# Longformer attention and a StarReLU MLP on one core: K and Q turned by DMA transposes from batch 2 on, V's global rows by register-indexed casting loads

## The chip, the cores and the metric

The kernel runs on one core of one Trainium2 chip. The time is the device time of one launch in microseconds, given as the median over runs. The engines are named as in the profile: PE (TensorE matmul), PEld (its weight loads), DVE (VectorE), ACT (ScalarE), POOL (GpSimd) and SP (SyncE). SP computes nothing; it issues DMAs. POOL issues DMAs as well. PE's results land in PSUM, in the kernel's pools `ps_s`, `ps_o` and `ps_m`; all other tiles lie in SBUF.

## The reference

Attention over 8 batches x 8 heads x 576 positions x 64 dims, restricted to a band of 32 positions on each side and to 8 global positions, which see all and are seen by all. Its output is the input of a two-layer MLP with a squared ReLU.

```python
scores = (1 / sqrt(64)) * q @ k.T                 # q, k, v: (8, 8, 576, 64) float32
mask = (abs(i - j) <= 32) | is_global[i] | is_global[j]
attn = softmax(where(mask, scores, -1e9))
x = (attn @ v).transpose(0, 2, 1, 3).reshape(4608, 512)
r = maximum(x @ w_in, 0)                          # w_in: (512, 2048)
out = (s * r * r + b) @ w_out                     # w_out: (2048, 512), float32 out
```

## The kernel before

**Pairs and chunks.** Two heads of a batch form a *pair*; there are 32 pairs, four to a batch (`bi, hp = divmod(p, 4)`). The two heads lie in the two halves of 64 partitions. The 576 keys are cut into `NCH` = 5 chunks of `KC` = 120; ahead of each chunk stand the 8 global keys, so a chunk has 128 columns. A chunk's keys meet only the queries in the band around it, 160 or 192 columns per head (`LO`, `HI`, `W`), plus the global queries.

**K and Q before.** `load_kq` has POOL issue two casting DMAs per pair, which put six neighbouring rows on a partition (`six[t]`, bf16, a ring of `NR` = 6 pairs). `trans_a` (K) and `trans_b` (Q) turn them with 12 PE transposes each into a PSUM tile `pst` (L392). DVE copies K to `kt` (L403) and one half of Q to `qbd` (L416), ACT the other half of Q (L416). `put_kq` then writes the global columns, two small DVE copies (L375 into `kt`, L379 into `qbd`).

**V before.** `load_v` brings V's natural rows in float32 to `natv` (a ring of `NV` = 4 pairs), from POOL for the first pairs and from SP after that; `cast_v` rounds them into `vring` (ACT up to pair 7, POOL afterwards, L166). The 8 rows of each chunk that belong to the global keys are filled by `put_v` (DVE up to pair 7, POOL afterwards, L368) from `gvx`.

**Global rows before.** Once per two batches, `gather` has POOL issue three indirect DMAs (L228) that fetch the global rows of K, Q and V into `gf`. `globals_of` gives five steps for them: round K and Q to `gb` (L334), turn them on PE (L341, then L344 and L347 on DVE), round V (L352), and two steps `move`, in which 8 matmuls with slices of the identity bring V's rows to partitions 0 to 7 (L359, then the copy to `gvx`, L361).

**The order of the work.** The program is written out by hand: `tc.manual_schedule` keeps each engine's order as recorded, and the engines run in order. Pairs 0 to 3 go through `first_pair`. From pair 4 on `run_pair` takes a pair through eight steps. In each step the functions left in `later` by the step before are taken aside as `prev`, and at its end one *quantum* of the MLP is issued:

- steps 0 to 4: `qk` (scores on PE, L427; exp on ACT, L431; the product with the mask, `em`, on DVE, L434, left in `later`). Steps 1 and 3 also take one of the two normalising functions of the pair before (L484, L488 on ACT; L471 and L490 on DVE).
- step 6: `trans_a` and `trans_b` of the next pair, then `pv` (weighted V into `po` and row sums, L453), and `put_v` of the next pair.
- at the end of each step:

```python
            for f in extra.get(s, ()):
                f()
            for f in prev:
                f()
            Q(nq[s])
```

So an *extra* of a step is issued ahead of the functions left by the step before it. A quantum is either the psh matmuls of one 128-row block of the first layer (L523, then ReLU on ACT, L530, and the square on DVE, L533) or a quarter of a second-layer output tile (L538, with L552 or L549 on DVE and a store on SP after every fourth). 16 psh quanta and 16 pso quanta make one of nine tiles of 512 tokens. Two pairs of a batch carry psh quanta, two carry pso quanta, eight in each pair (six in pairs 4 to 7). What is left of the MLP runs after pair 31. `scatter` (POOL, L501) writes the global queries' outputs into `xt` once per batch. `wpiece` and the adds of L705 build a bias row in pairs 8 to 15, and `release` (L716) adds it to eight output tiles that were held back.

DMAs of one queue carry eight semaphores in turn, so that a DMA waits until the eighth before it on its queue has landed.

Of the kernel before, what the change touches and what calls it, by code (L numbers as in the profile page):

```python
# [9 lines left out]
FP32 = mybir.dt.float32  # L10
BF16 = mybir.dt.bfloat16
# [5 lines left out]
P = 128  # L17
B, H, S, D = 8, 8, 576, 64
NG = 8
# [8 lines left out]
NCH = 5  # L28
KC = 120
HB = 60  # L30
LQ = NCH * P
# [1 line left out]
HI = [P * c + P + WIN for c in range(NCH - 1)] + [LQ]  # L33
W = [HI[c] - LO[c] for c in range(NCH)]
NPAIR = B * H // 2
NR = 6
NV = 4
NJ = 6
NP6 = S // NJ
N6 = NCH * KC // NJ  # L40


# [8 lines left out]
def view(ap, *dims):  # L51

    return bass.AP(
        tensor=ap.tensor, offset=ap.offset, ap=[list(ap.ap[0])] + [list(d) for d in dims]
    )
# [8 lines left out]
def kernel(  # L64
# [12 lines left out]
    nc = tc.nc  # L77
# [5 lines left out]
    const = ctx.enter_context(tc.tile_pool(name="const", bufs=1))  # L83
# [5 lines left out]
    gpa = ctx.enter_context(tc.tile_pool(name="gpa", bufs=1))  # L89
    held = ctx.enter_context(tc.tile_pool(name="held", bufs=1))  # L90
    mop = ctx.enter_context(tc.tile_pool(name="mop", bufs=3))
    stage = ctx.enter_context(tc.tile_pool(name="stage", bufs=3))
    globp = ctx.enter_context(tc.tile_pool(name="globp", bufs=2))
    ps_s = ctx.enter_context(tc.tile_pool(name="ps_s", bufs=2, space=bass.MemoryType.PSUM))
    ps_o = ctx.enter_context(tc.tile_pool(name="ps_o", bufs=1, space=bass.MemoryType.PSUM))
# [11 lines left out]
            name=nc.get_next_instruction_name(), act_func_set_id=_set_id,  # L107
# [9 lines left out]
        out=gidx_p[:],  # L117
# [6 lines left out]
    src = {"k": k, "q": q, "v": v}  # L124

    six = {t: const.tile([P, NR, 2, NJ, D], BF16, name=f"six{t}", tag=f"six{t}") for t in "kq"}
    natv = const.tile([P, NV, NCH, 2, D], FP32)
    vring = const.tile([P, NV, NCH, 2, D], BF16)
    qbufs = [const.tile([P, 2, LQ], BF16, name=f"qbd{i}", tag=f"qbd{i}") for i in range(3)]
# [10 lines left out]
    def load_kq(p):  # L140
        bi, hp = divmod(p, 4)
        for t in "kq":
            nc.gpsimd.dma_start(  # L143
                out=six[t][:NP6, p % NR].rearrange("p h j d -> p h (j d)"),
                in_=src[t][bi, 2 * hp : 2 * hp + 2].rearrange("h (p j) d -> p h (j d)", j=NJ),
            )

    def load_v(eng, p):
        bi, hp = divmod(p, 4)
        for hh in range(2):  # L150
            o = v[bi, 2 * hp + hh, 0, 0].offset

            last = p == NPAIR - 1 and hh == 1
            for c, nch, n in ((0, NCH - 1, KC), (NCH - 1, 1, S - KC * (NCH - 1))) if last else (
                (0, NCH, KC),
            ):
                eng.dma_start(
                    out=natv[NG : NG + n, p % NV, c : c + nch, hh],
                    in_=bass.AP(
                        tensor=v.tensor, offset=o + c * KC * D,  # L160
                        ap=[[D, n], [KC * D, nch], [1, D]],
                    ),
                )

    def cast_v(eng, p):
        eng(out=vring[:, p % NV], in_=natv[:, p % NV])  # L166
# [11 lines left out]
    clear(natv[0:NG].rearrange("p n c h d -> p (n c h d)"), NV * NCH * 2 * D)  # L178
    for t in "kq":
        nc.vector.memset(six[t][NP6:P, :, :, NJ - 1], 0.0)  # L180
    for t in gqd:
        nc.vector.memset(t[0:D, 1], 0.0)
        nc.vector.memset(t[D:P, 0], 0.0)
# [40 lines left out]
    def gather(bb):  # L224

        gfs[bb] = globp.tile([P, 3, D], FP32, tag="gf", name="gf")
        for i, t in enumerate("kqv"):
            nc.gpsimd.indirect_dma_start(  # L228
                out=gfs[bb][:, i], out_offset=None,
                in_=src[t].rearrange("b h s d -> (b h s) d"),  # L230
                in_offset=IndirectOffsetOnAxis(ap=grow[bb][:], axis=0),
            )
# [94 lines left out]
    def globals_of(bb):  # L327

        gb = globp.tile([P, 3, D], BF16, tag="gb", name="gb")
        gkt[bb] = globp.tile([P, D], BF16, tag="gkt", name="gkt")  # L330
        gvx[bb] = globp.tile([NG, 8, 2, D], BF16, tag="gvx", name="gvx")

        def round_kq():
            nc.vector.tensor_copy(out=gb[:, 0:2], in_=gfs[bb][:, 0:2])  # L334

        def turn():
            ps = ps_m.tile([P, 2, D], BF16, tag="moe", name="psg")
            for i in range(2):
                for hh in range(2):
                    r = slice(D * hh, D * hh + D)  # L340
                    nc.tensor.transpose(ps[r, i], gb[r, i], ident[r, r])  # L341

            def evac():
                nc.vector.tensor_copy(out=gkt[bb][:], in_=ps[:, 0])  # L344
                for hh in range(2):
                    r = slice(D * hh, D * hh + D)
                    nc.vector.tensor_copy(out=gqd[bb % 2][r, hh], in_=ps[r, 1])  # L347

            later.append(evac)

        def round_v():
            nc.vector.tensor_copy(out=gb[:, 2], in_=gfs[bb][:, 2])  # L352

        def move(i):
            ps = ps_m.tile([P, 4, 2, D], FP32, tag="moe", name="psv")
            for hp in range(4):
                for hh in range(2):
                    r0 = D * hh + 32 * i + NG * hp
                    nc.tensor.matmul(ps[:NG, hp, hh], ident[:, r0 : r0 + NG], gb[:, 2])  # L359
            later.append(  # L360
                lambda: nc.vector.tensor_copy(out=gvx[bb][:, 4 * i : 4 * i + 4], in_=ps[:NG])  # L361
            )

        return round_kq, turn, round_v, lambda: move(0), lambda: move(1)

    def put_v(eng, p):
        bb, x = divmod(p, 8)
        eng(  # L368
            out=vring[0:NG, p % NV].rearrange("g c h d -> g c (h d)"),
            in_=view(gvx[bb][:, x], [0, NCH], [1, 2 * D]),  # L370
        )

    def put_kq(p):
        bb, x = divmod(p, 8)
        nc.vector.tensor_copy(  # L375
            out=view(ktile[p][:], [P, NCH], [1, NG]),
            in_=view(gkt[bb][:, NG * x : NG * x + NG], [0, NCH], [1, NG]),
        )
        nc.vector.tensor_copy(  # L379
            out=view(qbufs[p % 3][:, 0, HB:], [LQ, 2], [P, NCH], [1, NG]),  # L380
            in_=view(gqd[bb % 2][:, 0, NG * x :], [D, 2], [0, NCH], [1, NG]),
        )
# [15 lines left out]
    def trans_a(p):  # L398
        ps = trans("k", p)
        kt = ktp.tile([P, LQ], BF16, tag="kt", name="kt")  # L400
        ktile[p] = kt
        later.append(
            lambda: nc.vector.tensor_copy(  # L403
                out=view(kt[:, NG:], [P, NCH], [NJ, KC // NJ], [1, NJ]),
                in_=view(ps[:], [KC // NJ, NCH], [1, KC // NJ], [NP6, NJ]),
            )
        )
# [175 lines left out]
    def run_pair(p, nq, extra):  # L583

        bi, hp = divmod(p, 4)
        more = p + 1 < NPAIR
        if hp == 0:
            open_batch(bi)
        for s in range(8):
            prev, later[:] = list(later), []  # L590
            if s < NCH:
                qk(p, s)
                if s in (1, 3):
                    step()
                if s == 2 and more:
                    cast_v(A if p < 7 else G, p + 1)
            elif s == 5:
                if hp == 0 and bi > 1:
                    later.append(lambda: scatter(bi - 1))
            elif s == 6:  # L600
                if more:
                    trans_a(p + 1)
                    trans_b(p + 1)
                pv(p)
                pending.extend(norm_steps(p))
            if s == 6 and more:
                put_v(V if p < 7 else G, p + 1)
            for f in extra.get(s, ()):
                f()
            for f in prev:  # L610
                f()
            Q(nq[s])
# [79 lines left out]
    load_w_out(3)  # L692
    load_kq(7)
    load_v(nc.gpsimd, 7)
    onesf = const.tile([P, P], FP32)
    nc.vector.memset(onesf[:], 1.0)
    quanta[0] = 32
# [22 lines left out]
    for p in range(4, NPAIR):  # L720
        bi, hp = divmod(p, 4)
        nq = [1] * 8
        if bi == 1:
            nq = [0, 1, 1, 1, 0, 1, 1, 1] if hp else [0, 0, 1, 1, 1, 1, 1, 1]
        elif hp == 0:
            quanta[0] += 32
        if p + 4 < NPAIR:
            load_kq(p + 4)
        if p >= 5 and p + 3 < NPAIR:
            load_v(nc.sync, p + 3)  # L730
        if p % 8 == 4 and p + 4 < NPAIR:
            gather((p + 4) // 8)
        ex = {}
        if p % 8 == 7 and p + 1 < NPAIR:
            for s, f in enumerate(globals_of((p + 1) // 8)):
                ex.setdefault(s, []).append(f)
        if 8 <= p < 15:
            for s in (4, 7):
                if adds:
                    ex.setdefault(s, []).append(adds.pop(0))  # L740
        if 7 <= p < 15:
            adds.extend(wpiece(p - 7))
        if p == 15:
            ex.setdefault(2, []).append(lambda: [f() for f in adds] and adds.clear())
            ex[2].append(bias)
        if p > 15 and held_rows:
            ex.setdefault(4, []).append(release)
            ex.setdefault(7, []).append(release)
        run_pair(p, nq, ex)
    flush()  # L750
    while pending:
# [39 lines left out]
```

## Time and profile before

| | us |
|---|---|
| median of 4 runs | 397.08 (396.43 to 397.66) |
| the profiled execution | 396.66 |
| its span, first to last instruction | 394.9 |
| pairs 7 to 30, first L427 to first L427 | 243.2 |
| from the last pair's first L427 to the end | 75.2 |

Busy times of the engines in parts of the loop, from the trace (us of 40, and mean DMA share):

| window | PE | DVE | ACT | POOL | DMA share |
|---|---|---|---|---|---|
| 50 to 90 | 36.2 | 29.0 | 26.0 | 19.1 | 0.88 |
| 130 to 170 | 35.8 | 32.0 | 21.2 | 15.2 | 0.40 |
| 170 to 210 | 36.7 | 32.3 | 23.4 | 17.1 | 0.59 |
| 250 to 290 | 38.3 | 28.6 | 24.5 | 11.5 | 0.46 |

A line of the timeline gives the start and duration in us, the engine, the source line, the operation, what it writes and reads, the shape and a count; a bracket gives the engine's idle time before it and what ended that. Matmuls are pipelined and their ends are modelled, so durations of neighbours overlap; their starts show how long PE is held.

### The profile page before, as it was taken

Reading aid. Unit: us, or ns where it says so; the run is one execution under the profiler, and the core shown is the slowest. Engines: PE = TensorE matmul, PEld = TensorE weight load, DVE = VectorE, ACT = ScalarE, POOL = GpSimd, SP = SyncE. Lnnn points to the kernel's source line nnn. Section 1 sums busy time; section 2 is a strip of 40 time slices with the busy share of each in tenths; the row PEclk is TensorE's granted clock in tenths of the full one; section 3 lists DMA queues with packets and bytes.
Section 4 is the critical chain, followed back from the end, with each engine's and each line's share of the span. In section 5 each row is a group of like instructions: output and inputs, shape, how many; then the busy total and the mean of one; then the engine's idle time right before and its main releaser. Section 6 shows DMA issues by size and latency. Waiting matters only on the chain.

```text
span 394.9 us, 9048 instructions
## 1 busy us (share of the span) xinstructions
PE 352.5 (89%) x3505; PEld 208.7 (53%) x3533; DVE 262.6 (66%) x648; ACT 216.2 (55%) x416; POOL 128.4 (33%) x224
## 2 busy tenths in 40 slices
PE   6675498899899979898899998999999999999996
PEld 2342344455555656456655784577556654544442
DVE  5864557787887888778776777687667763432431
ACT  5766468745674557346854685467746761630710
POOL 7753287047750650329501800292004001000000
PEclk9955589999999999999999999999999999999999
DMA  5999499755970380159533930584021002001002
GB/s 96 186 209 197 76 177 184 148 105 94 230 150 10 65 167 2 35 159 175 113 103 111 191 49 2 116 166 74 2 85 55 2 0 82 29 27 66 15 27 80
DMA packets 56558, 38.07 MB, mean 96 GB/s; under 512 B 34792, under 2 KB 49128, under 8 KB 56516
## 3 DMA queue, kind: packets, MB, share of 16 engines
q0 software_dynamic: 18784, 20.07, 30.1%
q1 hardware_dynamic: 37732, 17.43, 17.5%
q8 instruction: 27, 0.44, 0.5%
q14 instruction: 15, 0.12, 0.1%
HBM read 41.68 MB, written 9.44 MB: 129 GB/s over the span
## 4 chain that ended last, share of the span: by engine, by line
PE 62%; DVE 19%; ACT 12%; issue 4%; DMA 2%; ACTq 0%; DVEq 0%; POOLq 0%
PE pso L538 30%; PE psh L523 17%; PE po L453 6%; PE pss L427 5%; DVE g L533 5%; ACT r L530 4%; DVE em L434 3%; PE pst L392 3%; ACT qbd L416 3%; DVE xt L490 3%; DVE qbd L416 2%; DVE kt L403 2%; ACT e L431 2%; DVE wsum L705 2%; DMA sixk<-in_k_dram 2%
## 5 line engine op out<-in xcount | busy, mean ns | idle before, releaser
L523 PE MATMUL psh<-xt,win_t 128*128 128x512 bf16 (+7 forms) x1020 | 140.4, 287 | 0.6 <-issue 0.5
L538 PE MATMUL pso<-wout_t,g 128*128 128x512 bf16 x553 | 132.5, 379 | 4.5 <-issue 2.2
L530 ACT ACTIVATE r<-psh 128x512 bf16<-128x512 f32 x144 | 87.6, 625 | 66.2 <-PE psh L523 63.9
L523 PEld LDWEIGHTS <-win_t 128*128 128x128 bf16 x1024 | 85.4, 98 | 48.3 <-issue 5.4
L431 ACT ACTIVATE e<-pss 128x384 bf16<-128x384 f32 (+1 forms) x160 | 76.3, 482 | 35.0 <-PE pss L427 31.9
L533 DVE TENSOR_TENSOR g<-r 128x512 bf16<-128x512 bf16 x144 | 64.7, 453 | 43.0 <-ACT r L530 41.5
L538 PEld LDWEIGHTS <-g 128*128 128x128 bf16 x576 | 54.5, 98 | 65.3 <-issue 5.1
L434 DVE TENSOR_TENSOR em<-e,mask 128x384 bf16<-128x384 bf16 (+1 forms) x160 | 61.3, 385 | 20.2 <-ACT e L431 19.7
L427 PE MATMUL pss<-qbd,kt 128*128 128x384 bf16 (+1 forms) x160 | 51.6, 332 | 20.5 <-ACT qbd L416 16.4
L501 POOL COPY xt<-xg 128x4 bf16 x64 | 14.4, 226 | 122.7 <-DVE xt L490 119.1
L416 ACT COPY qbd<-pst 64x600 bf16<-64x600 bf16 x32 | 20.9, 654 | 54.3 <-DVE qbd L416 54.1
L552 DVE SCALAR_TENSOR_TENSOR osb<-pso,s_bc,bias_row 128x512 f32<-128x512 f32 x28 | 20.9, 747 | 37.4 <-PE pso L538 37.4
L368 POOL COPY vring<-gvx 8x640 bf16<-8x640 bf16 x24 | 18.5, 771 | 54.7 <-DVE gvx L361 53.4
L427 PEld LDWEIGHTS <-kt 128*128 128x128 bf16 x160 | 15.5, 99 | 30.1 <-DVE qbd L379 11.9
L490 DVE TENSOR_TENSOR xt<-po,rep 128x600 bf16<-128x600 f32 x32 | 24.9, 779 | 4.8 <-ACT rep L488 4.6
L453 PE MATMUL po<-em,vring 128*64 128x160 bf16 (+3 forms) x448 | 21.4, 229 | 6.6 <-DVE xt L490 6.3
L403 DVE COPY kt<-pst 128x600 bf16<-128x600 bf16 x32 | 24.8, 774 | 3.6 <-PE pst L392 3.6
L484 ACT ACTIVATE ln<-po 128x640 f32<-128x640 f32 x32 | 22.5, 705 | 5.1 <-PE po L453 5.1
L416 DVE COPY qbd<-pst 64x600 bf16<-64x600 bf16 x32 | 24.5, 765 | 1.2 <-PE pst L392 1.2
L488 ACT ACTIVATE rep<-ln 128x640 f32<-128x640 f32 x32 | 24.2, 757 | 0.1
L143 POOL DMA_DIRECT2D sixk<-in_k_dram x32 | 21.3, 666 | 6.6 <-issue 5.7
L453 PEld LDWEIGHTS <-vring 128*64 128x64 bf16 x448 | 17.8, 115 | 9.8 <-DVE xt L490 5.6
(81 smaller groups left out, 268.2 us busy)
## 6 DMA issues: line engine op xcount, KB each, us to landing
natv<-in_v_dram SPq DMA_DIRECT2D x51, 150.0 KB, 5.0
out_dram<-osb SPq DMA_DIRECT2D x28, 256.0 KB, 2.0
sixk<-in_k_dram POOLq DMA_DIRECT2D x32, 144.0 KB, 4.9
sixq<-in_q_dram POOLq DMA_DIRECT2D x32, 144.0 KB, 5.3
wst<-in_moe_w_out_dram POOLq DMA_DIRECT2D x8, 512.0 KB, 7.0
win_t<-in_moe_w_in_dram POOLq DMA_DIRECT2D x2, 1024.0 KB, 11.5
wout_t<-in_moe_w_out_dram POOLq DMA_DIRECT2D x4, 512.0 KB, 8.6
out_dram<-osbh SPq DMA_DIRECT2D x8, 256.0 KB, 2.1
```

The lines of the kernel that those rows point to most:

```text
L403: lambda: nc.vector.tensor_copy(out=view(kt[:, NG:], [P, NCH], [NJ, KC // NJ], [1, NJ]), in_=view(ps[:], [KC // NJ, NCH], [1, KC // NJ], [ ...
L416: eng(out=view(qbufs[p % 3][r, hh], [P, NCH], [HB + NG, 2], [NJ, n], [1, NJ]), in_=view(ps[r], [2 * n, NCH], [n, 2], [1, n], [NP6, NJ]),)
L427: nc.tensor.matmul(ps[:], ktile[p][:, P * c : P * c + P], qbufs[p % 3][:, :, LO[c] : HI[c]])
L431: nc.scalar.activation(e[:], ps[:], AF.Exp, scale=SCALE)
L434: later.append(lambda: nc.vector.tensor_mul(em[:], e[:], masks[c]))
L453: nc.tensor.matmul(po[D * hh : D * hh + D, a : a + n], onesb[:] if part else vring[:, p % NV, c, hh], emt[(p, c)][:, hh, x : x + n], start ...
L488: nc.scalar.activation(rep[:], ln[:], AF.Exp, scale=-1.0)
L490: lambda: nc.vector.tensor_tensor(out=xt[:, hp].rearrange("p (c a j) -> p c a j", c=NCH, a=2), in0=halves(po[:, 0:LQ]), in1=halves(rep[:]) ...
L523: nc.tensor.matmul(psh[:, d0 : d0 + n], win_t[:, a, f * P : f * P + P], xts[bi][:, a, x0 : x0 + n], start=(a == 0 and j == 0), stop=(a == ...
L530: nc.scalar.activation(r[:], psh[:], AF.Relu)
L533: later.append(lambda g=g, r=r: nc.vector.tensor_mul(g[:], r[:], r[:]))
L538: nc.tensor.matmul(pso[:], gl[f][:, u * P : u * P + P], wout_t[:, f], start=(f == 0), stop=(f == 15),)
```

## The change

From pair 8 on (`NSIX` = 8) K and Q are loaded by SP as natural float32 rows (`load_nat`), two DMAs for K and four for Q per pair, into rings of four pairs. ACT rounds them to `natb` (`round_nat`, step 5 for K and step 7 for Q, two pairs ahead), SP issues one DMA transpose of 128x1280 bf16 behind that (`turn_nat`, step 7), and `place_nat`, an extra of step 5 one pair ahead, copies the Q half into `qbd` with two DVE copies and calls `put_kq`. The K half is used where the transpose puts it. V's loads all go to SP.

For batches 2 to 7, V's global rows come by eight casting DMAs on POOL with a register-indexed source into `gvall`, issued once, ahead of pair 4's `gather`; `gather` fetches K and Q only for those, and `globals_of` gives two steps, which move to step 7 of pair 5 (13, 21) and step 1 of pair 6 (14, 22). `put_v` is on DVE throughout. `release` is called once per pair instead of twice, and the rings `NR` and `stage` are one shorter.

```diff
+    def load_nat(eng, t, p):
+        bi, hp = divmod(p, 4)
+        dst = natv if t == "v" else nat[t]
+        parts = ((0, 0, HB), (HB, HB, HB)) if t == "q" else ((NG if t == "v" else 0, 0, KC),)
+        for hh in range(2):
+            o = src[t][bi, 2 * hp + hh, 0, 0].offset
+            for r, a, n in parts:
...
+                for c, nch, m in runs:
+                    eng.dma_start(
+                        out=dst[r : r + m, p % NV, c : c + nch, hh],
+                        in_=bass.AP(
+                            tensor=src[t].tensor, offset=o + (c * KC + a) * D,
+                            ap=[[D, m], [KC * D, nch], [1, D]],
+                        ),
+                    )
+    def round_nat(i, t, p):
+        nc.scalar.copy(
+            out=natb[p % 2][0:KC, i].rearrange("p (c h d) -> p c h d", c=NCH, h=2),
+            in_=nat[t][0:KC, p % NV],
+        )
+    def turn_nat(p):
+        kqt[p] = kqp.tile([P, QT0 + NCH * P], BF16, tag="kqt", name="kqt")
+        nc.sync.dma_start_transpose(
+            out=kqt[p][:, KT0:].rearrange("p (c x) -> p c x", x=P),
+            in_=natb[p % 2][:].rearrange("p t x -> p (t x)"),
+        )
+    def place_nat(p):
+        ktile[p] = kqt[p][:, KT0 - NG : KT0 - NG + LQ]
         for hh in range(2):
+            r = slice(D * hh, D * hh + D)
+            nc.vector.tensor_copy(
+                out=view(qbufs[p % 3][r, hh], [P, NCH], [HB + NG, 2], [1, HB]),
+                in_=view(kqt[p][r, QT0:], [P, NCH], [HB, 2], [1, HB]),
+            )
+        put_kq(p)
...
-        for i, t in enumerate("kqv"):
+        for i, t in enumerate("kq" if bb else "kqv"):
...
+        g = gvx[0][:, 2 * D * p :] if p < 8 else gvall[:, 2 * D * (p - 8) :]
...
-                if more:
+                if p + 1 < NSIX:
                     trans_a(p + 1)
                     trans_b(p + 1)
...
-                put_v(V if p < 7 else G, p + 1)
+                put_v(V, p + 1)
...
+    gvall = const.tile([NG, (B - 2) * H * D], BF16)
+    for i in range(NG):
+        nc.gpsimd.dma_start(
+            out=gvall[i : i + 1].rearrange("o (b h d) -> o b h d", b=B - 2, h=H),
+            in_=v[2:, :, ds(greg_p[i], 1), :].rearrange("b h o d -> o b h d"),
+        )
...
         if p + 4 < NPAIR:
-            load_kq(p + 4)
-        if p >= 5 and p + 3 < NPAIR:
-            load_v(nc.sync, p + 3)
+            for t in "kqv":
+                load_nat(nc.sync, t, p + 4)
...
+        if p >= 6 and p + 2 < NPAIR:
+            at(5, round_nat, 0, "k", p + 2)
+            at(7, round_nat, 1, "q", p + 2)
+            at(7, turn_nat, p + 2)
+        if p % 8 > 4 and p + 3 < NPAIR:
+            if p % 8 == 5:
+                steps = globals_of((p + 4) // 8)
+                at(7, steps[0])
+            elif p % 8 == 6:
+                at(1, steps[1])
+        if p >= 7 and p + 1 < NPAIR:
+            at(5, place_nat, p + 1)
```

## The prediction

> **What bounds the kernel now.** I read the page first: the span is 394.9 us, and the slices of part 2 show TensorE (PE) at 9 tenths from slice 6 on.
>
> ```profile
> PE 352.5 (89%) x3505; PEld 208.7 (53%) x3533; DVE 262.6 (66%) x648; ACT 216.2 (55%) x416; POOL 128.4 (33%) x224
> PE   6675498899899979898899998999999999999996
> ```
>
> The change works between pair 5 and pair 31, so I cut the timeline at the first score matmul (L427) of each pair. Pairs 7 to 30 run from 76.52 to 319.72 us: 243.2 us for 24 pairs. Pairs whose eight steps hold pso matmuls take 9.26 us (pair 19: 201.16 to 210.42) with PE busy nearly all of it; pairs with psh matmuls take 9.99 us undisturbed (pair 30) and up to 11.9. So PE bounds the loop, but the lines at a pair's end show what stands right behind it (timeline, pair 19; columns are start, duration, engine, line, operation):
>
> ```profile
> 205.72 0.78 DVE L490 TENSOR_TENSOR xt<-po,rep 128x600 bf16<-128x600 f32 x1 [0.26 <-ACT rep L488]
> 206.42 0.74 DVE L552 SCALAR_TENSOR_TENSOR osb<-pso,s_bc,bias_row 128x512 f32<-128x512 f32 x1
> 207.08 0.31 DVE L434 TENSOR_TENSOR em<-e,mask 128x320 bf16<-128x320 bf16 x1
> ...
> 207.19 0.45 PE L392 MATMUL pst<-ident,sixk 96*64 96x96 bf16 x12
> ...
> 207.48 0.42 PE L392 MATMUL pst<-ident,sixq 96*64 96x96 bf16 x12
> ...
> 207.74 0.59 PE L453 MATMUL po<-em,vring 128*64 128x160 bf16 x14
> ...
> 207.91 0.77 DVE L403 COPY kt<-pst 128x600 bf16<-128x600 bf16 x1
> ```
>
> The reader is to see two things. The 24 transposes hold PE only from 207.19 to 207.74, 0.55 us; their summed durations are longer because they overlap. And VectorE (DVE) finishes the fifth mask product em at 207.39, 0.2 us after PE became free: the transposes cover that lateness.
>
> The second place is the start of the loop, on the POOL queue:
>
> ```profile
> 50.13 1.56 POOL L312 DMA_DIRECT2D wout_t<-in_moe_w_out_dram  x2
> 51.65 0.71 POOL L143 DMA_DIRECT2D sixk<-in_k_dram  x1
> ...
> 52.95 1.89 POOL L157 DMA_DIRECT2D natv<-in_v_dram  x2
> ...
> 57.55 1.18 POOL L228 DMA_INDIRECT gf<-in_k_dram,grow  x1 [1.37 <-DMA wout_t<-in_moe_w_out_dram]
> 61.13 1.00 POOL L228 DMA_INDIRECT gf<-in_q_dram,grow  x1 [2.41 <-DMA wout_t<-in_moe_w_out_dram]
> ```
>
> The two gathers wait for weight loads that they do not read: each DMA of this queue waits until the eighth before it has landed. By the trace's landings wout_t land at 57.3 and 60.9 and the last natv at 64.06.
>
> **What the Trainium skill says.** "VectorE: DVE Perf Modes", The three transpose paths: a crossbar DMA transpose of one 128x128 bf16 block takes 1309 ns; "Advanced Engine Details and Errata", X-Bar Transpose (TRN2): such DMAs reach 350 to 400 GB/s. The trace has none. "VectorE: DVE Perf Modes", Rules for kernel authors: a dense bf16 copy inside SBUF gets four elements per cycle; the trace's nearest row, vring<-gvx (8x640, L368), takes 468 ns on DVE, about half of the PSUM copy's rate per element (600 in 774 ns), so twice the rate, not four times. "SBUF — State Buffer", SBUF: two separate sides: GpSimd and DVE exclude each other on a shared port pair. The trace agrees: em of 384 columns takes 0.36 us, but 0.86 to 0.88 at 180.7 to 185.5, beside a burst of POOL casts, copies and DMA issues.
>
> **The change, part by part.** All against the profiled execution: 396.66 us, of which 394.9 are span.
>
> *Transposes off PE.* 24 pairs x 0.55 us = 13.2 us of PE time go, and with them DVE's kt and qbd copies (0.77 each, L403, L416) and ScalarE's (ACT) qbd copy (0.65). In their place place_nat puts two copies of 600 bf16 from SBUF on DVE. Price: on the rate of the vring<-gvx row, 0.13 + 600 x 0.53 ns = 0.44 us each; bounds 0.29 (four per cycle) and 0.77 (the kt row). They stand in step 5 *ahead of* em, with the two small copies (L375, L379) behind them. DVE operations follow each other some 0.08 us sooner than their durations, so em moves by 2 x 0.36 + 0.18 = 0.90 us. In pair 19 it would end at 208.29. PE, free at 207.19, runs the four chunks of po that are ready (0.35), waits to 208.34, needs 0.52 more, then two steps of 0.87: the next pair starts at 210.60 instead of 210.42. **The gain of 0.55 turns into a loss of 0.2**, for 12 pso pairs +2.4 us. With 0.29 per copy it is -0.1, with 0.77 +0.85. In pair 30 the same sum (em from 316.00, PE free at 315.82) gives 319.53 instead of 319.72, because PE's wait of 0.49 for qbd also goes; but ACT is given two roundings (0.73 each, as L166) for one copy of 0.65, +0.8 us where it has 8.0 us of work. I take 0 for the 12 psh pairs, bounds -0.5 and +0.5 each.
>
> *put_v on DVE* from pair 8 on (0.47 each): behind em, where DVE no longer has kt and qbd to do. Cost nothing while PE's two steps cover it; uncovered it would be 24 x 0.47 = 11 us.
>
> *V's global rows.* 16 psv matmuls, two gvx copies and a gb cast go from pairs 7, 15 and 23. Pair 23 takes 11.31 us against 9.26 for its like; keeping 0.2 for the K and Q part (moved to pairs 21 and 22) the gain is 1.8. Pair 15 the same, pair 7 nothing measurable (8.68, with six steps): -3.6 us.
>
> *POOL relief.* POOL loses 24 put copies (0.77) and 48 K and Q issues (0.66). In pairs 13, 17, 21 and 25 em sums to 3.1 to 3.2 us against 1.7. The three casts of each burst stay, so I take a third, 4 x 0.5 = -2 us; bounds 0 and -6.
>
> *The gathers behind gvall.* Eight gvall DMAs now stand ahead of gather(1) on POOL, and its use, the gb cast, moves from pair 7 to step 7 of pair 5, on DVE *ahead of* kt and qbd for pair 6. The eighth gvall waits for the natv that landed at 64.06; with 0.95 for its issue (as natv, L157) and 0.30 ahead of each gather the K gather issues at 65.3 and the Q gather at 66.7; landing takes 5.3 (part 6): 72.0. DVE stands ready at 65.0, after g and ahead of kt (64.97). So DVE, all masks and both copies queued behind gb, and PE, which waits for them, stand 7 us. SP also loads K and Q of pairs 9 and 10 just then, 0.6 MB more; at the 154 GB/s of that window (50 to 90 us) up to 3.9 us later. I take **8.5 us**, bounds 5 and 12. Nothing later gives it back, since PE has no idle time to fill.
>
> *SP's queue.* Per pair: two K, four Q, two V loads, one transpose. Issue 0.5 us each as natv, 4 to 5 us of a 9.5 us pair; stores (0.37) stand between. Casting loads leave POOL's queue. Cost nothing, as loads come two pairs ahead; if not, ACT waits in round_nat. Early K and Q of pair 8 and two more clears: +0.5, bounds 0 and 1.5.
>
> *The transpose itself.* 128x1280 bf16, 0.33 MB. From below: a store's 2.0 us from issue to landing plus 0.9 at 350 GB/s, about 3; from above ten blocks of 1.309 plus 2, about 15. Nearest in kind are natv's 600 rows of 256 bytes, 5.0 us; I take 5. The time there is: in a psh pair ACT's second rounding ends about where the next pair starts, and DVE reaches place_nat 6 us later; after pso pairs, where ACT has no relu, nearly 9 us. So 5 is hidden; above 6 every excess stops DVE in 12 pairs, above 9 in all.
>
> Sum: 2.4 + 0 - 3.6 - 2 + 8.5 + 0.5 = +5.8 us, so 402.5 against 396.66 (what follows pair 31 is not touched); the median of the runs shown, 397.08, stands 0.4 above that execution, so **403.0 us**.
>
> **Rivals.** *Late transposes* (0.22): at 8 us, 12 pairs x 2 = +24, 427 us; at 15 us, 12 x 9 + 12 x 6 = +180. For: one block alone is priced at 1.3 us, and the loads share the 16 engines. Against: the rate, and DMA shares of 0.40 to 0.61 in the loop. *A gain* (0.17), the other sign: place copies at 0.29 us (12 x -0.1, and psh pairs at -0.4 each), relief of 4, and a stall of only 5: -1.2 - 4.8 - 3.6 - 4 + 5 + 0.5 = -8, 389 us. It decides where a place copy falls under 0.35 us. For: the skill's rate. Against: the vring<-gvx row and the order of the queue. *The sums cancel* (0.06): within 0.8 us (0.2%, about what a measurement of this kernel can tell from no change).
>
> **How the numbers follow.** Forecast 0.55: all of it slower, since the parts with their bounds leave +1 to +12, 398 to 409. Faster 0.17, same 0.06, slower 0.55 + 0.22 = 0.77. The range 392 to 428 leaves out the better half of the gain and the worse half of the late transposes.
>
> **What would show it.** Right: DVE gb waits some 8 us for gf near 65 us; PE po waits for DVE em in pso pairs; place copies near 0.44; pairs 19 and 30 near 9.5 and 10. Wrong: gb without a wait; pairs under 9 us; or qbd<-kqt waiting for the transpose, which would be the first rival.

## The result, and the profile after

The changed kernel takes 398.73 us (median of 38 runs) against 396.89 us for the kernel before (59 runs): a ratio of 1.0043, 95% interval 1.0033 to 1.0053. It is slower by 0.4%, where 1.5% was forecast. The profiled execution of the changed kernel took 399.73 us, 397.8 of them span: 3.07 us more than that of before. Medians are over all executions; the ratios leave out a few in a slower state, over 1.5% above the fastest of their kernel. The page, parts 1 to 3:

```profile
PE 341.1 (86%) x2881; PEld 198.0 (50%) x2909; DVE 240.5 (60%) x665; ACT 228.4 (57%) x440; POOL 79.7 (20%) x157
...
PE   6676397499998899799989999999999999999995
...
PEclk9856589599999999999999999999999999999999
...
q1 hardware_dynamic: 128975, 40.04, 57.2%
```

PE lost 11.4 us of work, DVE 22 and POOL 49, and the span still grew. A hole of PE stands in slices 7 and 8 (60 to 80 us), which read 7 and 4 where they read 8 and 8 before; from slice 9 on the two rows are much alike. PE's granted clock, in tenths, reads 5 in slice 8, where it was 9 before. The packets of q1, the queue of SP's loads and stores, went from 37732 to 128975 and their share of the DMA engines from 17.5% to 57.2%. The table cuts the span at the first score matmul of each pair, as the prediction did (us, from the timeline):

| stretch | before | after | difference |
|---|---|---|---|
| start of the span to pair 7 | 76.52 | 86.25 | +9.73 |
| 12 psh pairs (9, 10, 13, 14, ... 30) | 127.19 | 120.77 | -6.42 |
| 9 pso pairs (8, 11, 12, 16, ... 28) | 83.33 | 86.45 | +3.12 |
| pairs 15 and 23 | 24.00 | 21.03 | -2.97 |
| pair 7 | 8.68 | 8.02 | -0.66 |
| pair 31 to the end | 75.2 | 75.3 | +0.1 |

The timeline of the changed kernel, the end of pair 19, which answers to the lines shown of before:

```profile
210.10 0.78 DVE L538 TENSOR_TENSOR xt<-po,rep 128x600 bf16<-128x600 f32 x1 [0.27 <-ACT rep L536]
210.80 0.74 DVE L600 SCALAR_TENSOR_TENSOR osb<-pso,s_bc,bias_row 128x512 f32<-128x512 f32 x1
211.46 0.69 DVE L199 COPY qbd<-kqt 64x600 bf16<-64x600 bf16 x2
211.57 0.51 PE L501 MATMUL po<-em,vring 128*64 128x160 bf16 x10
212.16 0.17 DVE L423 COPY kqt<-gkt 128x40 bf16<-128x40 bf16 x1
212.25 0.18 DVE L427 COPY qbd<-gqd 128x80 bf16<-128x80 bf16 x1
212.34 0.32 DVE L482 TENSOR_TENSOR em<-e,mask 128x320 bf16<-128x320 bf16 x1
...
212.70 0.28 PE L501 MATMUL po<-em,vring 128*64 128x32 bf16 x4 [0.62 <-DVE em L482]
```

PE is at po at 211.57 without any transposes ahead of it, does the ready chunks and stands until em ends at 212.66. Four small copies are on DVE between osb and em. The 0.55 us that PE saved is spent waiting.

The waits of the changed kernel (engine, line, releaser: sum in us, times, longest) show that PE stands for em in all 24 pairs, and show the other loss:

```profile
PE po L501 <- DVE em L482: 19.1, 24, 1.2
...
DVE gb L377 <- DMA gf<-in_q_dram,grow: 7.0, 1, 7.0
```

The timeline of the start, POOL's queue and what waits behind it:

```profile
63.93 0.52 POOL L745 DMA_DIRECT2D gvall<-in_v_dram  x1 [3.88 <-DMA wout_t<-in_moe_w_out_dram]
...
68.21 0.52 POOL L745 DMA_DIRECT2D gvall<-in_v_dram  x1 [0.56 <-DMA natv<-in_v_dram]
69.03 1.03 POOL L270 DMA_INDIRECT gf<-in_k_dram,grow  x1 [0.30 <-issue]
70.36 0.99 POOL L270 DMA_INDIRECT gf<-in_q_dram,grow  x1 [0.30 <-DMA natv<-in_v_dram]
...
72.93 0.23 DVE L377 CAST gb<-gf 128x128 bf16<-128x128 f32 x1 [7.01 <-DMA gf<-in_q_dram,grow]
73.08 0.78 DVE L451 COPY kt<-pst 128x600 bf16<-128x600 bf16 x1
...
75.27 0.75 PE L475 MATMUL pss<-qbd,kt 128*128 128x320 bf16 x2 [7.45 <-ACT qbd L464]
```

From the third on, each gvall waits for the eighth DMA before it. So the two gathers come 9 to 12 us later than before, gb stands for them, kt and qbd stand behind gb, and PE's score matmul behind both.

### The profile page after: what moved, and what is told of

It is laid out like the page before. It is cut to its first block, busy times and chain, and to the rows that moved or that the text cites. A ratio compares the mean times of both kernels' runs of the same rounds, so it can differ in the third digit from the quotient of the medians.

```text
span 397.8 us, 8007 instructions
## 1 busy us (share of the span) xinstructions
PE 341.1 (86%) x2881; PEld 198.0 (50%) x2909; DVE 240.5 (60%) x665; ACT 228.4 (57%) x440; POOL 79.7 (20%) x157
## 3 DMA queue, kind: packets, MB, share of 16 engines
q1 hardware_dynamic: 128975, 40.04, 57.2%
## 4 chain that ended last, share of the span: by engine, by line
PE 46%; DVE 22%; ACT 14%; issue 9%; DMA 7%; POOL 1%; ACTq 0%; DVEq 0%; POOLq 0%
PE pso L586 22%; PE psh L571 13%; PE po L501 6%; ACT r L578 6%; DVE xt L538 4%; ACT rep L536 3%; PE pss L475 3%; DVE qbd L199 3%; DVE em L482 3%; DVE g L581 3%; ACT e L479 2%; DMA gvall<-in_v_dram 2%; DMA natv<-in_v_dram 2%; DVE osb L600 2%; DMA sixk<-in_k_dram 2%
## 5 line engine op out<-in xcount | busy, mean ns | idle before, releaser
L578 ACT ACTIVATE r<-psh 128x512 bf16<-128x512 f32 x144 | 90.0, 627 | 62.3 <-PE psh L571 60.3
L479 ACT ACTIVATE e<-pss 128x384 bf16<-128x384 f32 (+1 forms) x160 | 76.6, 484 | 67.8 <-PE pss L475 64.9
L482 DVE TENSOR_TENSOR em<-e,mask 128x384 bf16<-128x384 bf16 (+1 forms) x160 | 54.7, 343 | 19.2 <-ACT e L479 18.4
L501 PE MATMUL po<-em,vring 128*64 128x160 bf16 (+3 forms) x448 | 25.4, 234 | 24.2 <-DVE em L482 19.1
L475 PE MATMUL pss<-qbd,kqt 128*128 128x384 bf16 (+1 forms) x120 | 37.8, 315 | 0.0
L475 PE MATMUL pss<-qbd,kt 128*128 128x384 bf16 (+1 forms) x40 | 14.4, 401 | 19.2 <-ACT qbd L464 15.2
L206 POOL CAST vring<-natv 128x640 bf16<-128x640 f32 x24 | 18.3, 779 | 24.1 <-DMA natv<-in_v_dram 18.7
L501 PE MATMUL po<-em,onesb 128*64 128x160 bf16 (+2 forms) x448 | 21.2, 231 | 0.0
L182 ACT CAST natb<-natk 120x640 bf16<-120x640 f32 x24 | 18.3, 763 | 0.0
L182 ACT CAST natb<-natq 120x640 bf16<-120x640 f32 x24 | 17.4, 726 | 0.0
L199 DVE COPY qbd<-kqt 64x600 bf16<-64x600 bf16 x48 | 16.1, 336 | 0.8 <-DMA kqt<-natb 0.5
```

Of the source, the lines that this page charges most:

```text
L182: nc.scalar.copy(out=natb[p % 2][0:KC, i].rearrange("p (c h d) -> p c h d", c=NCH, h=2), in_=nat[t][0:KC, p % NV],)
L475: nc.tensor.matmul(ps[:], ktile[p][:, P * c : P * c + P], qbufs[p % 3][:, :, LO[c] : HI[c]])
L479: nc.scalar.activation(e[:], ps[:], AF.Exp, scale=SCALE)
L482: later.append(lambda: nc.vector.tensor_mul(em[:], e[:], masks[c]))
L501: nc.tensor.matmul(po[D * hh : D * hh + D, a : a + n], onesb[:] if part else vring[:, p % NV, c, hh], emt[(p, c)][:, hh, x : x + n], start ...
L578: nc.scalar.activation(r[:], psh[:], AF.Relu)
```

## The experiments

Each ratio is against the kernel before on the same chip. Where a number is given against the changed kernel, it is a difference of medians or of the same pairs in two traces. "em sums to" means the five mask products of a pair together.

**1. Gathers ahead of gvall.**

```diff
-    for i in range(NG):
-        nc.gpsimd.dma_start(
...
         if p % 8 == 4 and p + 4 < NPAIR:
             gather((p + 4) // 8)
+            if p == 4:
+                for i in range(NG):
+                    nc.gpsimd.dma_start(
...
```

> The changed kernel with one move: the eight gvall loads are issued behind the two gathers of K's and Q's global rows in place of ahead of them. Own theory (the gathers stood in POOL's queue behind gvall, and DVE's gb cast stood 7.0 us for them, PE with it): the gb wait goes, pair 5 takes about 9.4 us in place of 16.3 and pair 6 about 9.1 in place of 11.0, in all 7 to 9.5 us less, about 390 us. Rival (the loads of natural rows that SP starts in these microseconds delay whatever lands then, so the gathers stay late): gb still waits 4 us or more, under 4 us less in all.

Measured: 394.8 us, 0.9938 (0.9916 to 0.9961), 3.9 less than the changed kernel; half of what my theory gave. The answer for the tile gf between 40 and 90 us:

```profile
L270 POOL DMA_INDIRECT gf<-in_k_dram,grow x1: 1040/1040/1040, 57.1 to 57.1; - x1
...
  DMA gf<-in_q_dram,grow: 1.6, 1
...
DMA to landing us min/median/max: 10.6/11.0/11.4
```

The gathers issue 12 us sooner and land in 11 us, where they took 5.0 to 7.9 in the kernel before and 2.5 in the changed one. So both theories hold a part: the queue order cost most of the wait, and early gathers are slow among the other loads. Pair 5 is still 11.8 us, pair 6 10.5.

**2. Placing copies behind em.**

```diff
             for f in prev:
                 f()
+            for f in extra.get(s + 0.5, ()):
+                f()
...
-            at(5, place_nat, p + 1)
+            at(5.5, place_nat, p + 1)
```

> The changed kernel with one move: the four placing copies of step 5 stand on DVE behind the fifth mask product em in place of ahead of it. Own theory (the copies hold up em and with it PE, which waits 19.1 us for em in 24 pairs, 0.8 each): pso pairs fall from 9.54 to about 8.7 us, psh pairs from 9.9 to 10.1 to about 9.2, in all 24 x 0.8 = 19 us less, about 380 us. Rival (the wait takes another form: scores of the next pair wait for the copies, or ScalarE with its two roundings sets psh pairs): under 8 us less, and the first score matmul of a pair waits for DVE.

Measured: 379.26 us, 0.9547 (0.9519 to 0.9575), 19.5 us less than the changed kernel. Pso pairs take 8.74 us, psh pairs 8.97 to 9.34 (pair 14 9.81). The timeline of this run, end of pair 19:

```profile
200.34 0.74 DVE L600 SCALAR_TENSOR_TENSOR osb<-pso,s_bc,bias_row 128x512 f32<-128x512 f32 x1
201.00 0.31 DVE L482 TENSOR_TENSOR em<-e,mask 128x320 bf16<-128x320 bf16 x1
201.12 0.61 PE L501 MATMUL po<-em,vring 128*64 128x160 bf16 x14
201.24 0.69 DVE L199 COPY qbd<-kqt 64x600 bf16<-64x600 bf16 x2
...
203.82 0.30 PE L475 MATMUL pss<-qbd,kqt 128*128 128x320 bf16 x1
```

The 14 po matmuls run in one piece, and the copies end 1.6 us before the next pair's scores need them. The order on DVE alone decided between 0.28 us lost and 0.52 us won in a pso pair.

**3. V's copies back on POOL, and, in the kernel before, on DVE.**

```diff
-                put_v(V, p + 1)
+                put_v(V if p < 7 else G, p + 1)
```

> The changed kernel with one edit undone: from pair 8 on the copies of V's global rows into vring run on POOL again in place of DVE. It tells which part of POOL's lighter load made psh pairs 13, 17, 21 and 25 1.5 to 2 us shorter. Theory A (POOL's copies, three or four in a burst beside the casts, slowed em on DVE): em in these pairs sums to about 3 us again instead of 1.7, they take 11 to 12 us again, in all 3 to 6 us more. Theory B (it was the casting loads' issues on POOL): em stays at 1.7, and the time stays within 1 us, or falls a little since DVE does 24 copies of 0.47 us less.

Measured: 400.8 us, 1.0093 (1.0066 to 1.0121), 2.1 more than the changed kernel. Neither theory fits. em sums to 2.4 us in pairs 17, 21 and 25 (1.70 in the changed kernel), yet these pairs take what they took, 10.05, 10.06 and 9.85. Only pair 14 is much longer, 12.28 for 10.66.

The reverse edit in the kernel before:

```diff
-                put_v(V if p < 7 else G, p + 1)
+                put_v(V, p + 1)
```

> The kernel before with one edit of the change alone: from pair 8 on the copies of V's global rows into vring run on DVE in place of POOL. Theory A (POOL's copies slowed em): em in pairs 13, 17 and 25 falls from 3.1 to under 2.2 us, these pairs come to some 10.5, in all 2 to 5 us less. Theory B (the casting loads' issues slow em): em stays near 3, and with 24 copies of 0.47 us more on a DVE that these pairs wait for, the time is the same or up to 4 us more.

Measured: 394.44 us, 0.9934 (0.9913 to 0.9954). em falls in pairs 17, 21 and 25 (2.55, 2.78, 1.83) but not in 13; pairs 13, 17, 21 and 25 together are 2.3 us shorter, 10 and 14 each 0.39 longer. A part of the relief, theory A in kind.

**4. gb a pair later.**

```diff
-        if p % 8 > 4 and p + 3 < NPAIR:
-            if p % 8 == 5:
-                steps = globals_of((p + 4) // 8)
+        if p % 8 > 5 and p + 2 < NPAIR:
+            if p % 8 == 6:
+                steps = globals_of((p + 3) // 8)
                 at(7, steps[0])
-            elif p % 8 == 6:
+            elif p % 8 == 7:
                 at(1, steps[1])
```

> The changed kernel with one move: the cast gb of K's and Q's gathered rows, and the four transposes that follow it, stand a pair later (step 7 of pair 6 and step 1 of pair 7, and so in 14 and 22), gvall stays ahead of the gathers. Own theory (the stall was nothing but DVE meeting gb before the gathers had landed at 72.8 us; the 10.6 to 11.4 us that they took when they were moved forward were the rest): gb finds its data, pair 5 takes about 9.4 and pair 6 about 9.1 us, in all 8 to 9.5 us less than the changed kernel, about 390 us. Rival (SP's loads of natural rows make other data late too): another wait appears in pairs 5 to 7 and under 5 us are won.

Measured: 390.73 us, 0.9838 (0.9809 to 0.9867), 8.0 less than the changed kernel. Pairs 5 and 6 take 9.35 and 9.49, gb finds its data, with gvall still ahead of the gathers. So the stall was the use that came too soon.

**5. The casting loads back on POOL.** Their data is read by nobody.

```diff
             for t in "kqv":
                 load_nat(nc.sync, t, p + 4)
+            if p > 7:
+                load_kq(p + 4)
```

> The changed kernel with one cost put back: from pair 8 on POOL also issues the two casting loads of K and Q per pair, as the kernel before does, into buffers that nobody reads any more. Theory B (these issues are what slowed em and DVE in psh pairs): em sums to over 2.3 us in pairs 13, 17, 21 and 25, they take 11 us or more, in all 3 to 6 us more. Theory C (DVE has had less to do since the change, so a slower em is caught up before PE needs it): em is slower in these pairs but they stay near 10.05 us, in all under 2 us more.

Measured: 411.54 us, 1.0332 (1.0264 to 1.04); its executions range from 407.34 to 415.82 us and the profiled one is the longest, so I read only pairs in which no data was late. There em sums to 2.15 us in pairs 17, 21 and 25, and these take 10.32, 10.31 and 9.85, at most 0.27 more: the size that theory C gave (its reason is tried in number 7). The rest of the loss is another thing, which the answer for tile kqt shows:

```profile
  DMA kqt<-natb: 10.7, 4
...
DMA to landing us min/median/max: 3.4/7.1/12.0
```

With the additional traffic the transposes, 4.3 us in the changed kernel, come late: the first rival of the prediction, brought about.

**6. Both back.** The edits of the last run and of the first of number 3 together.

> The changed kernel with both costs put back: the unread casting loads of K and Q on POOL from pair 8 on, and the copies into vring on POOL, so that POOL has all it had before. Theory B' (POOL's load alone makes the psh pairs long): em near 3 us in pairs 13, 17, 21 and 25, these take 11 to 12 us as before, in all 5 to 8 us more. Theory C (POOL's load counts only beside DVE's two copies out of PSUM, 1.54 us a pair, which the change took away): em near 3 us, but the pairs under 10.6, in all under 3 us more.

Measured: 413.42 us, 1.0401 (1.0361 to 1.0441). em is 2.7 to 2.9 us in pairs 17, 21 and 25, but late kqt (8.2 us, 6 times) and late natv stand between: inconclusive. So the same was tried with less traffic:

```diff
+    def load_few(p):
+        bi, hp = divmod(p, 4)
+        for t in "kq":
+            nc.gpsimd.dma_start(
+                out=six[t][:NP6, p % NR, :, 0],
+                in_=src[t][bi, 2 * hp : 2 * hp + 2].rearrange("h (p j) d -> p h j d", j=NJ)[:, :, 0],
+            )
...
+            if p > 7:
+                load_few(p + 4)
...
-                put_v(V, p + 1)
+                put_v(V if p < 7 else G, p + 1)
```

> The changed kernel with POOL's load put back but not the traffic: from pair 8 on POOL issues two unread casting loads per pair with as many pieces as those of K and Q before, each of a sixth of the bytes, and POOL makes the copies into vring. Theory B' (POOL's load alone makes the psh pairs long): em sums to 2.7 us or more in pairs 17, 21 and 25 and these take 10.7 us or more, in all 4 to 7 us more than the changed kernel. Theory C (it counts only beside DVE's copies out of PSUM, which the change took away): em is as slow, but these pairs stay under 10.5 us, in all under 3 us more. DVE should wait for kqt no more than 2 us.

Measured: 406.92 us, 1.0252 (1.02 to 1.0305); the profiled execution is 5.9 us longer than that of the changed kernel. Pairs 7 to 30 take 244.18 us, against 236.28 in the changed kernel and 243.2 before. Pairs 14, 17, 21 and 25 take 14.73, 11.86, 11.82 and 10.70; pair 13 is unchanged. DVE waits for kqt in no pair. POOL's timeline in three kernels tells why. Before (pair 21 starts at 219.68):

```profile
215.82 2.20 POOL L501 COPY xt<-xg 128x4 bf16 x8 [20.13 <-DVE xt L490]
218.37 0.69 POOL L143 DMA_DIRECT2D sixk<-in_k_dram  x1 [0.35 <-issue]
...
225.44 0.73 POOL L166 CAST vring<-natv 128x640 bf16<-128x640 f32 x1
```

After (pair 21 starts at 224.62):

```profile
220.49 2.29 POOL L549 COPY xt<-xg 128x4 bf16 x8 [25.86 <-DVE xt L538]
222.71 2.04 POOL L206 CAST vring<-natv 128x640 bf16<-128x640 f32 x3
```

With POOL's load back (pair 21 starts at 228.49):

```profile
224.36 2.29 POOL L557 COPY xt<-xg 128x4 bf16 x8 [24.64 <-DVE xt L546]
226.81 0.70 POOL L159 DMA_DIRECT2D sixk<-in_k_dram  x1 [0.16 <-issue]
...
236.09 0.63 POOL L159 DMA_DIRECT2D sixq<-in_q_dram  x1
```

POOL's queue stands at the scatter (xt<-xg) until a batch is complete, while issues, casts and copies pile up behind it; then all run in one burst. Before, the burst reaches 6.5 us into pair 21 (10.26 us long), and 9.7 into pair 25 (10.74); after, it is over 0.1 us after the start of pair 21; with the load back it reaches 8.2 us into it. There DVE is slow (timeline, DVE, the same run):

```profile
231.80 0.90 DVE L589 TENSOR_TENSOR g<-r 128x512 bf16<-128x512 bf16 x1 [0.25 <-ACT r L586]
232.62 0.86 DVE L490 TENSOR_TENSOR em<-e,mask 128x384 bf16<-128x384 bf16 x1
...
234.87 0.86 DVE L490 TENSOR_TENSOR em<-e,mask 128x384 bf16<-128x384 bf16 x1
```

g takes 0.90 for 0.43 and em 0.86 for 0.36. In the run with V's copies alone on POOL the burst ends 2.5 us into pair 21 (10.06 us long): DVE catches up before PE needs the last em. So what counts is how far into the pair the burst reaches, not the number of POOL's operations. It is the casts and copies in it that slow em; beside a DMA issue alone em is hardly ever slow (counts in the last section). The issues push casts and copies into the pair.

Two things keep this from being the whole answer. First, 4.07 of the 7.9 us that the loop lost fall to pair 14, which took 10.18 in the kernel before. PE stands there for DVE, and then runs at a granted clock of 0.50 from 161.0 to 167.8 us (the same run):

```profile
160.50 0.51 PE L509 MATMUL po<-em,vring 128*64 128x160 bf16 x10 [2.35 <-DVE xt L546]
```

Second, pair 13, which the change had shortened most (1.88 us), stayed short, and so did pair 9. In pairs 7 to 14 POOL also issues the `wst` loads into the ring `stage`, which the change made one shorter, and these wait longer for DVE's adds. POOL's waits for them before and after, then POOL's timeline after (pair 13 is 143.66 to 153.71):

```profile
POOL wst L701 <- DVE wsum L705: 4.7, 2, 2.4
...
POOL wst L755 <- DVE wsum L759: 22.9, 3, 9.0
...
153.35 0.72 POOL L755 DMA_DIRECT2D wst<-in_moe_w_out_dram  x1 [9.02 <-DVE wsum L759]
154.07 2.57 POOL L206 CAST vring<-natv 128x640 bf16<-128x640 f32 x3
```

Casts that ran in pair 13 before now run in pair 14, with the load back as well. Whether the lighter load or the shorter ring made pairs 9 and 13 shorter, no run separates.

**7. DVE's load back as well**, since theory C says that it decides. `one_more` is an addition of 600 float32 columns on DVE.

```diff
+            if s == 6 and 7 < p < NPAIR - 1:
+                later.append(one_more)
```

> The run with POOL's load put back, and one more operation on DVE in step 7 of each pair from 8 on (an addition of 600 columns into a buffer that nobody reads, about 0.7 us), so that DVE too has what it had before (1.54 us for kt and qbd before, 0.67 for the placing copies and 0.7 for this now). Theory C: psh pairs 13, 17, 21 and 25 take 10.7 to 12 us again, 0.5 to 0.8 us a pair more than without the addition, in all 3 to 6 us more than that run. Theory B': no pair is longer by more than 0.2 us than without the addition.

Measured: 408.05 us, 1.0293 (1.0235 to 1.0351); pairs 7 to 30 take 243.34 us, 0.8 less than without the addition, pairs 17, 21 and 25 11.37, 11.38 and 10.75. Theory C falls: 0.7 us more of DVE's work in step 7 costs nothing, and POOL's burst explains pairs 17, 21 and 25 without it.

**8. One release per pair, in the kernel before.**

```diff
             ex.setdefault(4, []).append(release)
-            ex.setdefault(7, []).append(release)
```

> The kernel before with one edit of the change alone: one held row is released per pair (step 4) in pairs 16 to 23 in place of two per pair in 16 to 19. Theory (each released row costs DVE 0.68 to 0.93 us, and psh pairs 17 and 18 stood on DVE): pair 18 falls from 11.0 to 10.2, pair 17 by 0.3 to 0.8, pairs 21 and 22 rise by at most 0.4, in all about 1 us less. Rival (the additions stand beside other work): nothing that can be measured.

Measured: 398.37 us, 1.0024 (1.0009 to 1.0039). Pair 18 falls by 1.0 to 9.99 as said, but pair 21 rises by 1.1, where an addition now stands in the burst (1.20 us for 0.68). Pair 17 rises by 0.5 with one addition fewer, and pair 10, ahead of the edit, by 0.6: a single pair can move by that much between two executions. This side edit of the change won nothing by itself.

**9. K's and Q's part alone.** V's third gather, psv matmuls and gvx copies are back for all batches, gvall is gone:

```diff
-        for i, t in enumerate("kq" if bb else "kqv"):
+        for i, t in enumerate("kqv"):
...
-        if bb:
-            return round_kq, turn
...
+        if p % 8 == 7 and p + 1 < NPAIR:
+            for s, f in enumerate(steps[2:]):
+                at(2 + s, f)
```

> The changed kernel with V's part undone: V's global rows of all batches come by the third gather, psv matmuls and gvx copies as in the kernel before (their copies into vring stay on DVE), and gvall is gone; gb stays in pair 5. It tells what V's part is worth alone. Own theory (without gvall the K and Q gathers issue near 57 and 58 us but land after some 11 us among SP's loads, as when they were moved forward, and the V matmuls come back in pairs 7, 15 and 23): the wait for gf falls from 7.0 to 1 to 3 us, pairs 15 and 23 rise by 1.2 and 1.8, in all about 398 us, within 1.5 us of the changed kernel. Rival (gvall was the whole stall): no wait for gf, 392 to 394 us.

Measured: 395.57 us, 0.9966 (0.9952 to 0.9981), 3.2 less than the changed kernel; gb waits 2.2 us. The time from pair 0's to pair 7's first score matmul is 4.8 us shorter, pairs 15 and 23 are 1.08 and 0.96 longer, pair 7 0.6. V's part wins 2.6 us in the loop and loses 4.8 at the start (pair 0 also came 1 us sooner in this execution).

**10. Both moves together.** The edits of numbers 2 and 4.

> The changed kernel with both moves that won time: the placing copies behind em, and gb a pair later. Own theory (the two losses lie in different stretches and add up: 19.5 and 8.0 us were won by each alone): 398.7 - 27.5 = 371 us, bounds 368 and 375, no wait of DVE for gf. Rival (shorter pairs leave the transposes and loads of natural rows too little time): DVE waits for kqt or POOL for natv more than 3 us in all, and 376 us or more.

Measured: 372.68 us, 0.9363 (0.9321 to 0.9405). It beats both kernels, by 24 us against the kernel before. The two gains nearly add (27.5 expected, 26.1 measured); DVE waits 3.3 us for kqt, and pair 14 takes 10.60, so the rival has begun to hold.

## Why the prediction was right or wrong

The sign was right, the size was not: +5.8 us was summed for the profiled execution and +3.07 came (+1.84 by the medians).

*The stall at the start: right in mechanism, in size partly by luck.* 9.0 was summed for it with the early loads, 9.73 came. gb waits 7.0 us for the Q gather, the 7 us of the working, and the names in the chain (gvall, gf, gb, kt, PE) are those of the timeline. Runs 1 and 4 show it from both sides. But two misses cancel in the 7 us: the Q gather issued at 70.36 where the working had 66.7, since the last natv ahead of it landed at 67.93 and not at 64.06, and it landed in 2.5 us where 5.3 was taken. The addition for later landings was put on the loads; what came beside the wait is mostly pair 6, 1.90 us longer than before, of which PE spent the first 4.7 us at half its clock, told below.

*Placing copies ahead of em: right in mechanism, a little small.* 12 x 0.2 = 2.4 was taken; pso pairs outside 15 and 23 lost 0.28 each, and pair 11 0.88, where a placing copy waits 0.5 us for its transpose and po 1.2 us for em. A copy took 0.34 us, not 0.44: between the two rates I had weighed (four elements per cycle by the Trainium skill, "VectorE: DVE Perf Modes", Rules for kernel authors, gave an estimate of 0.29). But the two copies take 0.69 us together, without the overlap of 0.08 us that the working subtracted from each. So em ends 7.12 us into pair 19 against 6.23 before: 0.89 later, where 0.90 was taken, by two misses that cancel. The rival "a gain" was to decide at copies under 0.35 us. They were, and no gain came in pso pairs: shorter copies did not free PE, since em is still behind them; PE waits 0.62 in pair 19, about the 0.55 it had saved. What the prediction did not say is that the same order costs as much in psh pairs; there another saving paid for it, and run 2 shows 0.8 to 0.9 us a pair in both kinds.

*POOL relief: the step that failed.* "The three casts of each burst stay, so I take a third, 4 x 0.5 = -2 us." In the changed kernel em sums to 1.70 us in pairs 13, 17, 21 and 25: all the slowness is gone, not a third, and these four pairs lost 4.60 us, nearer to the bound of -6 than to -2. The psh pairs together lost 6.42 us, where -2 and 0 were taken; this 4.4 us is larger than the whole error of 2.7, and the smaller misses (start +0.7, pso +0.7, V's rows +0.6, pair 7 -0.7) leave the difference. The fault was to share out a burst by the count of its operations. It is a queue that starts at a fixed event, the scatter, and the DVE work that it meets is set by when its casts and copies end. Without 48 issues and 24 copies it ends as the psh pair begins.

The runs show this for pairs 17, 21 and 25: they had lost 2.72 us by the change, and the run with POOL's load back (number 6) returned 4.43. V's copies alone or the issues alone lengthened them by no more than 0.27 each. For pairs 9, 13 and 18, which lost 1.21, 1.88 and 0.90, it is not shown, since they stayed short in that run. In 9 and 13 the shorter ring `stage` is a rival that no run tried. Pair 18 lost one of two releases, which took 1.0 from it by itself (number 8). That DVE and POOL slow each other is what the Trainium skill says ("SBUF — State Buffer", SBUF: two separate sides), and the 0.86 us for em agrees; what neither said is how much of it reaches PE.

*V's global rows: right in the sum.* -3.6 was taken; pairs 15 and 23 lost 2.97, or 3.5 without the 0.28 each that the placing copies cost there. Run 9 shows 2.04 of it to be V's part, and 0.6 in pair 7, where nothing was taken. The rest may be K's and Q's two steps, which the change moved to other pairs; no run separates them.

*Transposes: right, with less to spare than said.* 5 us was taken and 4.3 came; DVE waited 0.5 us in all, in pair 11. But the argument from DMA shares of 0.40 to 0.61 was wrong: K and Q as natural rows raised the share in pairs 7 to 30 from 0.44 to 0.88. Run 5, at 1.05, shows the transposes late.

## What to carry to other kernels

Where work is taken off the engine that bounds a kernel, look at what is queued ahead of the operation it then waits for: moving four copies behind one multiplication was worth 19.5 us, more than the change around it. Price a burst on a shared resource by when it starts and ends against the work beside it, and by which of its operations slow that work, not by their number. Before an early load is moved in a queue, ask first whether its use can be moved later: that took a wait of 7 us away at once, where the earlier issue won only half.

## What the runs showed of the hardware

- A stall of PE costs more than its length. In the changed kernel PE has no matmul from about 67.8 to 75.27 us, and the granted clock was 0.50 from 69.8 to 80.0; pair 6 took 10.98 us. With gb a pair later the clock was 1.00 from 68.6 to 86 us and pair 6 took 9.49. In run 6 a stall of 2.35 us was followed by a clock of 0.50 from 161.0 to 167.8. The Trainium skill ("TensorE: Matmul & The Clock Gate", Part 1: The HAM clock gate) says that PE falls to half its clock after an idle window of some 3.4 us and comes back after as long a busy one. The traces agree on the half and on a return some microseconds after PE begins again (4.7 and 7.3 us here), but the fall came about 2 us after the last matmul, and in run 6 after a stall shorter than 3.4 us. The sum of the prediction had no term for it.
- Of POOL's operations the casts and copies slow em on DVE, the DMA issues hardly. In the traces of both kernels and of runs 3, 5, 6 (with load_few) and 7, an em of 384 columns in pairs 8 to 30 took 0.34 to 0.36 us in all 390 cases with nothing on POOL beside it, 0.34 to 0.40 in 42 of 47 beside DMA issues alone, and 0.83 to 0.88 in all 20 beside a copy into vring.
- An indirect gather of 128 rows landed in 2.5 us at 69 us, in 5.0 to 7.9 in the kernel before, and in 10.6 to 11.4 at 57 us, beside SP's loads and behind V loads of POOL's own queue that took as long (12.1 and 12.4).
- A DMA transpose of 128x1280 bf16 landed 4.3 us after its issue (median of 24), 1.36 us of them on SP's queue. In run 5, at a DMA share of 1.05, the median was 7.1 and the longest 12.0 us.
